# Retention and a squared-ReLU FFN in one kernel: fewer DMAs for q and for a tail's store, and retention clusters joined from the sixth group on

## The chip, the cores and the metric

The kernel runs on one core of a Trainium2 chip. The metric is the device time in microseconds (us) of one execution, as the median of several. The core has five engines that work side by side: TensorE (PE in the profile) for matrix products into PSUM, VectorE (DVE), ScalarE (ACT), GpSimd (POOL), and SyncE (SP), which here issues nearly all DMA transfers. Sixteen DMA engines move the data between device memory (DRAM) and on-chip memory (SBUF). "SPq" and "ACTq" in the profile are the DMA issues of SyncE and ScalarE.

## The reference

A causal retention (attention without softmax, with a decay per head) feeds a feed-forward network (FFN) whose nonlinearity is the square of ReLU.

```python
# q, k, v: (8 sequences, 8 heads, 576 positions, 64), float32
scores = scale * np.matmul(q, k.transpose(0, 1, 3, 2))
gamma = 1.0 - 2.0 ** (-5.0 - np.arange(H))
Dmat = np.where(rel >= 0, gamma[:, None, None] ** rel[None, :, :], 0.0)
attn_out = np.matmul(scores * Dmat[None], v)
# x: (4608, 512); w_in: (512, 2048); w_out: (2048, 512)
x = attn_out.transpose(0, 2, 1, 3).reshape(B * S, H * D)
h = x @ w_in
r = np.maximum(h, 0.0)
out = (r * r) @ w_out
```

## The kernel before

A sequence of 576 positions is four full chunks of 128 and a tail of 64. A *unit* is one full chunk of one sequence, or the tails of two sequences together, on the 128 partitions. There are 36 units, and a *group* is two of them; the 18 groups are numbered from 0. The last group (17) and group 8 consist of tails; all others of full chunks. Groups 0 to 3 are loaded and transposed in another way (`PAIRED = 8` units) and are not touched by the change.

The host-side scheduler takes tasks with an engine, a priority key, an assumed duration and dependencies, runs an event simulation, and writes the instructions in the order that comes out. The order on each engine is then fixed: what an assumed duration changes is only that order.

```python
for t in self.tasks: ...          # event simulation, then: for t in order: t["fn"]()

units = []                        # per pair of sequences: 8 full units; after every second pair: 2 tail units
sizes = [2] * 18                  # groups
JOIN = 7
sched = Schedule(dict(ff=8, prS=1, prO=1, g=3, ld=5, wst=4, kq=7, v16=7, rT=2, x=3, rl=3, o=4, ..., kqT=6))
```

Loading a unit, and its casts and transpose. The q of a full unit is laid out so that partition 32 x + r has four consecutive rows of heads x and x + 4; k and v have a row per partition.

```python
def add_load(u):
    for n, (name, src) in enumerate((("k", k), ("q", q), ("v", v))):
        def fn(name=name, src=src):
            x = ld.tile([P, H, D], FP32, ...)
            if kind == "full" and name == "q":
                for j in range(NP):                                   # NP = 4
                    nc.sync.dma_start(out=x[32 * j:32 * j + 32].rearrange("r (a t) d -> r a (t d)", a=2),
                                      in_=src[b, :, c * P:(c + 1) * P, :].rearrange("(a x) (r t) d -> x r a (t d)", a=2, t=4)[j])
            elif kind == "full":
                nc.sync.dma_start(out=x, in_=src[b, :, c * P:(c + 1) * P, :].rearrange("h p d -> p h d"))
            ...
        loaded[name, u] = dma_task(0, QL if name == "q" and kind == "full" else 1.2, fn, ...)   # QL = 0.8

ck = add("POOL", base, 0.65, fk, deps=[loaded["k", u]], acq=("kq",))      # casts to float16
cq = add("POOL", base + 1, 0.62, fq, deps=[loaded["q", u], ck])
cv = add("POOL", base + 2, 1.1, fv, deps=[loaded["v", u]] + tail, acq=("v16",))
def fx2():
    t = tile_of["kqT", u] = work.tile([P, 2 * NP, P], FP16, ..., bufs=6)
    nc.sync.dma_start_transpose(out=t, in_=tile_of["kq", u].rearrange("p x n -> p (x n)"))
T["kqT", u] = [add("SP", -1, 2.7, fx2, deps=[ck, cq], acq=("kqT",), after=3.0, lag=LAG_T)]
```

The retention of a group on PE, as quads of 64x64 matmuls. A group not joined has a cluster with its scores and its sums (the state that is carried on) and a later cluster with its outputs. From group `JOIN` on a cluster holds the first outputs of a group and the scores of the next, and another the sums of the next and the rest of the outputs.

```python
def joined(g):
    return JOIN <= g < last_g

if not joined(g - 1):
    def fa():
        emit_scores(g)
        emit_sums(g)
    t = add("PE", base + 3, ..., fa, deps=scores_deps(g) + sums_deps(g), acq=(...))
if joined(g):
    def f1():
        emit_out1(g)
        emit_scores(g + 1)
    def f2():
        first_waits.append(tile_of["masking", g + 1])
        emit_sums(g + 1)
        emit_out2(g)
    t1 = add("PE", base + 10, ..., f1, deps=out1_deps(g) + scores_deps(g + 1), acq=("prO", "prS", "ff", "ff", "ff", "ff"))
    t2 = add("PE", base + 30, ..., f2, deps=[t1] + T["masked", g] + T["masked", g + 1] + sums_deps(g + 1), ..., lag=PAUSE)
else:
    def fb():
        emit_out1(g)
        nc.tensor.drain()
        emit_out2(g)
    t = add("PE", base + 24, ..., fb, deps=T["masked", g] + out1_deps(g), acq=("prO", "ff", "ff"))
```

`JOIN` also sets the priority of a group's casts on GpSimd: `base_of(g) - L * (2 if g > JOIN else 1)`, an earlier key for the groups after it.

Group g needs, for its scores, the transposed k and q (`kqT`) of both its units. The FFN of a group is 64 matmuls of 128x256 for the first product and 56 for the second (seven block products per group, from group 1 on). Its output is stored so:

```python
def store(u, o, lo=0, hi=DM, eng=nc.sync):
    if kind == "full":
        eng.dma_start(out=out[r0:r0 + P, lo:hi], in_=o[:, lo:hi])
    else:
        for i in range(2):
            r0 = (b + i) * S + 512
            eng.dma_start(out=out[r0:r0 + 64, lo:hi], in_=o[i * 64:(i + 1) * 64, lo:hi])
```

In the last group each unit is stored in two halves of 256 columns as they are done, one half by ScalarE's queue and one by SyncE's; the two units give four such stores. In group 8 a unit is one store of all 512 columns, issued by SyncE.

Of the kernel before, what the change touches and what calls it, by code (L numbers as in the profile page):

```python
# [15 lines left out]
class Schedule:  # L16
# [7 lines left out]
    def add(self, eng, key, dur, fn, deps=(), acq=(), after=None, lag=0.0):  # L24
        t = dict(eng=eng, key=key, dur=dur, fn=fn, acq=acq, n=len(self.tasks), users=[], free=[], lag=lag,
                 left=len(deps), ready=0.0, lat=self.LAT[eng] if after is None else after)
        for d in deps:
            d["users"].append(t)
        self.tasks.append(t)
        return t  # L30
# [73 lines left out]
def kernel(  # L104
# [9 lines left out]
    nc = tc.nc  # L114
    B, H, S, D = q.shape
    DM, DFF = w_in.shape
    assert (B, H, S, D, DM, DFF) == (8, 8, 576, 64, 512, 2048)
    P = 128
    NP = H // 2
# [84 lines left out]
    for kind, pattern in (("tail", [[1, 64]]), ("full", [[1, 4], [4, 16]])):  # L204
        m = mask[kind] = const.tile([P, 64], FP16, name=f"mask_{kind}")
# [7 lines left out]
    for c in range(2):  # L213
        for e in range(2):
            m = mask2[c * 64:(c + 1) * 64, e]
# [17 lines left out]
    WT_KEY = 96  # L233
    URGENT = 40
    SQ_LATE = (1, 4, 6)
    JOIN = 7
    LAG = {"k4": 0.7, "q4": 0.5}
    LAG_T, LAG_O = 1.5, 5.0
    PAIRED = 8
# [3 lines left out]
    add = sched.add  # L243
# [34 lines left out]
    def dma_task(key, dur, fn, **kw):  # L278
        t = add("SP", key, dur, fn, deps=list(last_load), **kw)
        last_load[:] = [t]  # L280
        return t
# [8 lines left out]
    def add_load(u):  # L290
        kind, b, c = units[u]
        for n, (name, src) in enumerate((("k", k), ("q", q), ("v", v))):
            def fn(name=name, src=src):
                x = ld.tile([P, H, D], FP32, name=f"{name}32", tag=f"{name}32")
                tile_of[name + "32", u] = x
                if kind == "full" and name == "q":
                    for j in range(NP):
                        nc.sync.dma_start(out=x[32 * j:32 * j + 32].rearrange("r (a t) d -> r a (t d)", a=2),
                                          in_=src[b, :, c * P:(c + 1) * P, :].rearrange("(a x) (r t) d -> x r a (t d)", a=2, t=4)[j])
                elif kind == "full":  # L300
                    nc.sync.dma_start(out=x, in_=src[b, :, c * P:(c + 1) * P, :].rearrange("h p d -> p h d"))
                else:
                    for i in range(2):
                        nc.sync.dma_start(out=x[i * 64:(i + 1) * 64],
                                          in_=src[b + i, :, 512:576, :].rearrange("h p d -> p h d"))
            loaded[name, u] = dma_task(0, QL if name == "q" and kind == "full" else 1.2, fn, acq=("ld",) if n == 0 else ())
# [42 lines left out]
    T = {}  # L349
# [15 lines left out]
    def add_unit(u, base):  # L365

        kind, b, c = units[u]
        tail = [tail_dec] if kind == "tail" else []

        def sorted_cast(op, out_, in_):  # L370
            op(out=out_.rearrange("p (n b a d) -> p n b a d", n=2, b=2, a=2),  # L371
               in_=in_.rearrange("p (a n b) d -> p n b a d", n=2, a=2))

        def fk():
            t = tile_of["kq", u] = cast.tile([P, 2, H * D], FP16, name="kq16", tag="kq16")
            sorted_cast(nc.gpsimd.tensor_copy, t[:, 0], tile_of["k32", u])

        def fq():
            if kind == "tail":
                sorted_cast(nc.gpsimd.tensor_copy, tile_of["kq", u][:, 1], tile_of["q32", u])  # L380
            else:
                nc.gpsimd.tensor_copy(out=tile_of["kq", u][:, 1].rearrange("p (t a d) -> p a t d", t=4, a=2),  # L382
                                      in_=tile_of["q32", u].rearrange("p (a t) d -> p a t d", a=2))

        def fv():
            t = tile_of["v16", u] = cast.tile([P, H, D], FP16, name="v16", tag="v16")
            nc.gpsimd.tensor_tensor(  # L387
                out=t, in0=tile_of["v32", u],
                in1=vdec[kind].rearrange("p (h o) -> p h o", o=1).to_broadcast([P, H, D]), op=ALU.mult)
        ck = add("POOL", base, 0.65, fk, deps=[loaded["k", u]], acq=("kq",))  # L390
        cq = add("POOL", base + 1, 0.62, fq, deps=[loaded["q", u], ck])
        cv = add("POOL", base + 2, 1.1, fv, deps=[loaded["v", u]] + tail, acq=("v16",))
        for what, t in (("k", ck), ("v", cv)):
            for w in gate.get((what, u), []):
                sched.need(w, t)
        T["casts", u] = [ck, cq, cv]
        sched.free("ld", [ck, cq, cv])
        def fx2():
            t = tile_of["kqT", u] = work.tile([P, 2 * NP, P], FP16, name="kqT", tag="kqT", bufs=6)
            nc.sync.dma_start_transpose(out=t, in_=tile_of["kq", u].rearrange("p x n -> p (x n)"))  # L400
        T["kqT", u] = [add("SP", -1, 2.7, fx2, deps=[ck, cq], acq=("kqT",), after=3.0, lag=LAG_T)]

    def add_unit_pair(u, base):

# [180 lines left out]
    def units_of(g):  # L585
        return sorted(groups[g])
# [4 lines left out]
    def base_of(g):  # L591
        return (units_of(g)[0] - len(groups[g])) * L - EARLY
# [81 lines left out]
    def joined(g):  # L674

        return JOIN <= g < last_g

# [83 lines left out]
    def add_casts(g):  # L761
        for u in units_of(g):
            if u < PAIRED:
                if u % 2 == 0:
                    add_unit_pair(u, base_of(g) - 5)
                continue
            add_unit(u, base_of(g) - L * (2 if g > JOIN else 1) + 4 * (u - units_of(g)[0]))

# [72 lines left out]
    def store(u, o, lo=0, hi=DM, eng=nc.sync):  # L841
        kind, b, c = units[u]
        if kind == "full":
            r0 = b * S + c * P
            eng.dma_start(out=out[r0:r0 + P, lo:hi], in_=o[:, lo:hi])
        else:
            for i in range(2):
                r0 = (b + i) * S + 512
                eng.dma_start(out=out[r0:r0 + 64, lo:hi], in_=o[i * 64:(i + 1) * 64, lo:hi])


    T["ff2"] = []
# [4 lines left out]
    def add_ff(g):  # L857
# [49 lines left out]
        for s, u in enumerate(us):  # L907
            end = base2 + NF * (s + 1)
            f2 = []
            late = g == 0 and s == 1  # L910
            for fi in range(NF):
                def f(fi=fi, s=s, u=u):
                    if fi == 0:
                        tile_of["po", u] = ps_ff.tile([P, DM], FP32, name="po", tag="ff")
                    nc.tensor.matmul(tile_of["po", u], lhsT=tile_of["g", g][:, fi, s * P:(s + 1) * P],  # L915
                                     rhs=w_out16[:, fi, :], start=(fi == 0), stop=(fi == NF - 1))
                f2.append(add("PE", 95.9 + fi / 1000 if late else base2 + NF * s + fi, 0.216, f, deps=[sq[fi // nf]] + wcast[4 + fi // 4] + f2[-1:],
                              acq=("ff",) if fi == 0 else ()))

            def fo(u=u):  # L920
                tile_of["o", u] = o_pool.tile([P, DM], FP32, name="o", tag="o")
                nc.scalar.copy(out=tile_of["o", u], in_=tile_of["po", u])
            oc = add("ACT", end + 1, 0.59, fo, deps=[f2[-1]], acq=("o",))
            sched.free("ff", [oc])
            st = add("SP", -0.5, 0.7, lambda u=u: store(u, tile_of["o", u]), deps=[oc], after=2.5, lag=LAG_O)
            sched.free("o", [st])
            ends.append(f2[-1])
# [3 lines left out]
    def add_strassen(g, us, base, sq):  # L931
# [124 lines left out]
        for u, ds in ((uA, [d11, c12]), (uB, [d22, d21])):  # L1056
            if g < last_g:
                st = [add("SP", -0.5, 0.7, lambda u=u: store(u, o_tile(u)), deps=ds, after=2.5, lag=LAG_O if g < last_g - 1 else 0.0)]
            else:
                st = []  # L1060
                for d in ds:
                    lo = 0 if d in (d11, d21) else HM
                    eng = ("ACT", base + 25.1, 0.05) if d is d11 or d is d22 else ("SP", -0.5, 0.05)
                    st.append(add(*eng, lambda u=u, lo=lo, eng=eng: store(u, o_tile(u), lo, lo + HM,
                                                                          nc.scalar if eng[0] == "ACT" else nc.sync),
                                  deps=[d], after=2.5))
            sched.free("o", st)
# [44 lines left out]
```

## Time and profile before

| | |
|---|---|
| time, median of 3 | 291.18 us (290.39 to 291.36) |
| span of the profiled execution | 288.7 us |
| DMA from SP: `k`, 24 issues of 256 KB | 4.5 us to landing (median) |
| DMA from SP: `q`, 96 issues of 64 KB | 3.2 us |
| DMA from SP: `v`, 24 issues of 256 KB | 3.4 us |
| transposes `kqT`, 28 issues | 3.9 us |
| stores of full units, 32 issues of 256 KB | 2.8 us |
| stores of tails, 4 of 128 KB and 8 of 64 KB | 3.1 us and 2.0 to 2.1 us |
| read and written | 36.70 MB and 9.44 MB |

The page has the busy share of each engine, the span in 40 equal slices (each digit is a tenth of busy time; for DMA it is the mean over 16 engines), the chain of work that ended last, and groups of instructions by line. In a row of the order of time the columns are start, duration (both us), engine, line of the kernel, operation, `out<-in`, shape, and how many instructions were merged into the row. Matmuls are pipelined, so the duration of a row is longer than its share of the engine's time; the distance from one start to the next is what counts.

The loads of the units from 8 on begin at about 42 us and the last transpose is issued at 221.63 us; PE's last block of matmuls starts at 283.35 us.

### The profile page before, as it was taken

What the parts mean: (1) busy time and instruction counts of PE and PEld (TensorE: products, weight loads), DVE (VectorE), ACT (ScalarE), POOL (GpSimd) and SP (SyncE); (2) the same over time, 40 slices, a digit from 0 to 9 for tenths busy, and PEclk for the clock granted to TensorE, in tenths of its full rate; (3) what the DMA queues carried; (4) which work ended last, traced back from release to release, by engine and by line L of the source; (5) the groups of instructions that cost most, each with busy time, mean ns of one, the idle gap of its engine ahead of it and who ended that gap; (6) DMA issues with size and microseconds to landing.
All of it is one profiled execution on the core that took longest, in us unless ns stands there. A gap on an engine that the chain in (4) does not pass through costs nothing.

```text
span 288.7 us, 10134 instructions
## 1 busy us (share of the span) xinstructions
PE 281.2 (97%) x4346; PEld 236.3 (82%) x4346; DVE 175.6 (61%) x341; ACT 187.6 (65%) x363; POOL 86.2 (30%) x124
## 2 busy tenths in 40 slices
PE   7999999999999999999999999999999999999994
PEld 2568767888888888888888888888888888888883
DVE  3772389858564857647474665666557656265632
ACT  5559975767575767667676757584867585847830
POOL 5560045443505233433434135252515000000000
PEclk9999999999999999999999999999999999999999
DMA  7999999999998797999989798969979120102004
GB/s 200 275 208 206 248 290 270 175 235 161 224 210 220 164 215 174 218 207 209 191 203 214 173 180 221 218 157 254 195 181 191 57 75 2 73 2 75 0 9 138
DMA packets 122156, 49.94 MB, mean 173 GB/s; under 512 B 94720, under 2 KB 117760, under 8 KB 122112
## 3 DMA queue, kind: packets, MB, share of 16 engines
q1 hardware_dynamic: 117568, 44.84, 70.3%
q0 software_dynamic: 4224, 4.19, 8.8%
q8 instruction: 34, 0.56, 0.8%
q10 hardware_dynamic: 320, 0.26, 0.4%
q14 instruction: 10, 0.08, 0.1%
HBM read 36.70 MB, written 9.44 MB: 160 GB/s over the span
## 4 chain that ended last, share of the span: by engine, by line
PE 91%; DMA 3%; POOL 2%; issue 2%; DVE 0%; POOLq 0%; DVEq 0%
PE ph L875 44%; PE po L972 36%; PE psO L357 4%; DMA w_in<-in_moe_w_in_dram 3%; PE po L915 2%; PE psc L357 2%; PE psS L357 2%; PE psT L439 1%; POOL mask L216 0%; POOL vx L420 0%; POOL w_in L331 0%; DVE o L995 0%; POOL mask_full L208 0%; POOL mask_tail L208 0%; DVE p L1024 0%
## 5 line engine op out<-in xcount | busy, mean ns | idle before, releaser
L875 PE MATMUL ph<-xT,w_in 128*128 128x256 f16 x1152 | 138.4, 273 | 0.1
L875 PEld LDWEIGHTS <-w_in 128*128 128x128 f16 x1152 | 111.4, 98 | 14.5 <-DMA w_in<-in_moe_w_in_dram 0.4
L883 ACT ACTIVATE rl<-ph 128x512 f16<-128x512 f32 x144 | 84.4, 587 | 56.5 <-PE ph L875 54.0
L893 ACT ACTIVATE gT<-rl 128x512 f16<-128x512 f16 x118 | 74.4, 631 | 3.4
L972 PEld LDWEIGHTS <-gS 128*128 128x128 f16 x544 | 51.7, 98 | 6.5
L972 PE MATMUL po<-wT,gS 128*128 128x256 f16 x408 | 55.9, 273 | 0.0
L972 PEld LDWEIGHTS <-gT 128*128 128x128 f16 x408 | 39.7, 98 | 4.7
L945 DVE TENSOR_TENSOR gS<-gT,gS 128x512 f16<-128x512 f16 (+1 forms) x51 | 28.6, 561 | 19.1 <-ACT gT L893 18.5
L972 PE MATMUL po<-w_out,gT 128*128 128x256 f16 x272 | 36.7, 273 | 0.0
L387 POOL TENSOR_TENSOR v<-v,vdec_full 128x512 f16<-128x512 f32 x24 | 26.2, 1090 | 24.5 <-DMA v<-in_v_dram 22.8
L945 DVE TENSOR_TENSOR gS<-gT 128x1024 f16<-128x1024 f16 x34 | 26.1, 769 | 10.9 <-ACT gT L893 9.4
L371 POOL CAST kq<-k 128x512 f16<-128x512 f32 x28 | 18.5, 661 | 47.3 <-DMA k<-in_k_dram 43.2
L382 POOL CAST kq<-q 128x512 f16<-128x512 f32 x24 | 16.1, 670 | 31.7 <-DMA q<-in_q_dram 31.7
L895 DVE TENSOR_TENSOR gT<-rl 128x512 f16<-128x512 f16 x26 | 12.0, 462 | 22.0 <-ACT rl L883 22.0
L995 DVE TENSOR_TENSOR o<-po,u 128x256 f32<-128x256 f32 x33 | 13.9, 422 | 17.3 <-ACT u L985 8.6
L985 ACT COPY u<-po 128x256 f32<-128x256 f32 x34 | 12.5, 368 | 13.6 <-PE po L972 13.5
L751 DVE TENSOR_TENSOR xT<-psO,gam_full 128x512 f16<-128x512 f32 x28 | 18.0, 682 | 3.7 <-PE psO L357 3.6
L995 DVE TENSOR_TENSOR o<-po,p 128x256 f32<-128x256 f32 x18 | 7.6, 424 | 20.6 <-ACT u L985 11.5
L972 PE MATMUL po<-w_out,gS 128*128 128x256 f16 x136 | 17.8, 273 | 0.0
L972 PE MATMUL po<-wT,gT 128*128 128x256 f16 x136 | 17.6, 273 | 0.0
L692 DVE TENSOR_TENSOR rT<-psc,mask_full 128x512 f16<-128x512 f32 x24 | 15.8, 684 | 2.2 <-PE psc L357 2.1
L461 DVE TENSOR_TENSOR R<-stmp,dec 128x512 f16<-128x512 f32 (+1 forms) x18 | 12.1, 671 | 0.4
(82 smaller groups left out, 220.8 us busy)
## 6 DMA issues: line engine op xcount, KB each, us to landing
out_dram<-o SPq DMA_DIRECT2D x32, 256.0 KB, 2.8
k<-in_k_dram SPq DMA_DIRECT2D x24, 256.0 KB, 4.5
q<-in_q_dram SPq DMA_DIRECT2D x96, 64.0 KB, 3.2
v<-in_v_dram SPq DMA_DIRECT2D x24, 256.0 KB, 3.4
pair<-in_k_dram SPq DMA_DIRECT2D x4, 512.0 KB, 5.7
pair<-in_q_dram SPq DMA_DIRECT2D x4, 512.0 KB, 7.3
pair<-in_v_dram SPq DMA_DIRECT2D x4, 512.0 KB, 6.8
w_in<-in_moe_w_in_dram POOLq DMA_DIRECT2D x4, 512.0 KB, 8.9
```

The source lines that it names most:

```text
L357: t = nc.tensor.matmul(out_, lhsT=lhsT, rhs=rhs, start=start, stop=True, skip_group_check=True, tile_position=(64 * row, 64 * col))
L371: op(out=out_.rearrange("p (n b a d) -> p n b a d", n=2, b=2, a=2), in_=in_.rearrange("p (a n b) d -> p n b a d", n=2, a=2))
L382: nc.gpsimd.tensor_copy(out=tile_of["kq", u][:, 1].rearrange("p (t a d) -> p a t d", t=4, a=2), in_=tile_of["q32", u].rearrange("p (a t) d ...
L387: nc.gpsimd.tensor_tensor(out=t, in0=tile_of["v32", u], in1=vdec[kind].rearrange("p (h o) -> p h o", o=1).to_broadcast([P, H, D]), op=ALU. ...
L692: tile_of["masking", g] = nc.vector.tensor_tensor(out=tile_of["rT", g][:, :, a], in0=tile_of["psc", g][a].rearrange("p (s n i) -> p s n i" ...
L751: nc.vector.tensor_tensor(out=tile_of["x", g].rearrange("p n (s e i) -> p e (n s) i", s=n, e=2)[:, c], in0=y.rearrange("p (o t r) -> p o r ...
L875: nc.tensor.matmul(tile_of["ph", g, fb][:, j, :], lhsT=w_in16[:, m, fi * P:(fi + 1) * P], rhs=tile_of["x", g][:, m, :], start=(m == 0), st ...
L883: nc.scalar.activation(out=t, in_=tile_of["ph", g, fb], func=ACTF.Relu)
L893: nc.scalar.activation(out=t, in_=rl, func=ACTF.Square)
L945: nc.vector.tensor_tensor(out=tile_of["S", g][:, k, sl], in0=in0(sl), in1=in1(sl), op=op)
L972: nc.tensor.matmul(tile_of["pb", g, bank], lhsT=left(i), rhs=right[:, i, :], start=(start and i == 0), stop=(i == HF - 1), skip_group_chec ...
L995: nc.vector.tensor_tensor(out=o_tile(u)[:, half * HM:(half + 1) * HM], in0=bank(x), in1=tile_of[name, g], op=ALU.add)
```

## The change

It has four parts. A tail's store becomes one DMA over both sequences and all 128 partitions, where it was one for each sequence. The q of a full unit becomes two DMAs, one for each half of the heads and over all partitions, where it was four of 32 partitions and all heads; the layout in SBUF is the same. The joined clusters begin with group 5, the sixth, in place of group 7. And the scheduler counts 2.4 us in place of 2.7 for a transpose. It is meant to spare issues on the DMA queues, and to spare the dearer separate clusters on PE.

```diff
-    JOIN = 7
+    JOIN = 5
@@ add_load
                 if kind == "full" and name == "q":
-                    for j in range(NP):
-                        nc.sync.dma_start(out=x[32 * j:32 * j + 32].rearrange("r (a t) d -> r a (t d)", a=2),
-                                          in_=src[b, :, c * P:(c + 1) * P, :].rearrange("(a x) (r t) d -> x r a (t d)", a=2, t=4)[j])
+                    for a in range(2):
+                        nc.sync.dma_start(out=x[:, NP * a:NP * a + NP].rearrange("p t d -> p (t d)"),
+                                          in_=src[b, NP * a:NP * a + NP, c * P:(c + 1) * P, :].rearrange("x (r t) d -> x r (t d)", t=4))
@@ add_unit
-        T["kqT", u] = [add("SP", -1, 2.7, fx2, deps=[ck, cq], acq=("kqT",), after=3.0, lag=LAG_T)]
+        T["kqT", u] = [add("SP", -1, 2.4, fx2, deps=[ck, cq], acq=("kqT",), after=3.0, lag=LAG_T)]
@@ store
-            for i in range(2):
-                r0 = (b + i) * S + 512
-                eng.dma_start(out=out[r0:r0 + 64, lo:hi], in_=o[i * 64:(i + 1) * 64, lo:hi])
+            eng.dma_start(out=out.rearrange("(b s) m -> b s m", s=S)[b:b + 2, 512:576, lo:hi], in_=o[:, lo:hi])
```

## The prediction, made before the result was known

> **What bounds the kernel now.** I read the page first: the share of each engine and the 40 slices.
>
> ```profile
> PE 281.2 (97%) x4346; PEld 236.3 (82%) x4346; DVE 175.6 (61%) x341; ACT 187.6 (65%) x363; POOL 86.2 (30%) x124
> ...
> PE   7999999999999999999999999999999999999994
> ...
> DMA  7999999999998797999989798969979120102004
> ...
> PE 91%; DMA 3%; POOL 2%; issue 2%; DVE 0%; POOLq 0%; DVEq 0%
> ```
>
> TensorE is full from the second slice to the last, and the chain of waits is 91% TensorE. A busy PE need not be at its peak, so I checked the order of time on PE. In the FFN blocks 20 matmuls of 128x256 start 2.18 us before the next block does, 109 ns each, and nearly every block follows the last one at that pace, from 17.7 us to 284.2 us. So only three things can move the end: what PE has to do, a wait put into its stream, and what comes after its last matmul. The DMA row is the second thing to see: about 9 tenths up to slice 31, nearly nothing after it. Loads run ahead of PE, but not at leisure.
>
> Second, the retention clusters on PE, in the order of time. Here a cluster of scores and sums that stands by itself (two L357 lines), then the FFN blocks on both sides of the same group's output cluster (its many short lines are left out):
>
> ```profile
> 90.73 1.04 PE L972 MATMUL po<-wT,gS 128*128 128x256 f16 x8
> 91.70 0.44 PE L357 MATMUL psc<-kqT 64*64 64x64 f16 x32
> 91.97 0.46 PE L357 MATMUL psS<-v,kq 64*64 64x64 f16 x32
> 92.37 0.61 PE L972 MATMUL po<-wT,gS 128*128 128x256 f16 x4
> ...
> 95.00 2.35 PE L875 MATMUL ph<-xT,w_in 128*128 128x256 f16 x20
> ...
> 98.20 1.05 PE L972 MATMUL po<-wT,gS 128*128 128x256 f16 x8
> ```
>
> 90.73 plus 8 x 0.109 is 91.60, and the next FFN block starts at 92.37: the scores and sums cost 0.77 us. 95.00 plus 20 x 0.109 is 97.18, next block 98.20: the outputs cost 1.02 us. A joined group, by the same sum, costs 0.60 (cluster at 154.35) plus 0.87 (at 158.46).
>
> Third, the end, and the stores of the last group, from the DMA view of 283 to 288 us and the order of time after 284 us:
>
> ```profile
> DMA  0005960049889301794006954989849620000000
> ...
> q10 hardware_dynamic: 320, 0.26, 21.5%
> ...
> out_dram<-o ACTq DMA_DIRECT2D x4, 64.0 KB, 2.1
> ```
>
> ```profile
> 284.46 0.42 DVE L995 TENSOR_TENSOR o<-po,p 128x256 f32<-128x256 f32 x1
> 284.92 1.10 SPq L849 DMA_DIRECT2D out_dram<-o  x2
> ```
>
> The last add ends at 284.88, two stores are issued in 1.10 us, the last packet is written by about 287.1 (33 slices of 0.125 us), and the span ends at 288.7. The row q10 is the tail stores issued by ACT: 256 packets of 1 KB and 64 tiny ones in 21.5% of 16 engines x 5 us = 17.2 us, so about 67 ns of one DMA engine for each KB. A full store's 2 KB packets take 87 ns by the same sum over 281 to 283 us (69.5% of 32 us by 256).
>
> [...] about 0.1 us lies between a full-array block and the 64x64 quads (91.60 to 91.70).
>
> **The change, part by part.**
>
> JOIN from 7 to 5 turns the outputs of groups 5 and 6 and the scores of groups 6 and 7 from separate clusters into joined ones. Removed: 2 x (0.77 + 1.02) = 3.58 us. Added: 2 x (0.60 + 0.87) = 2.94 us. PE saves 0.6 us. All on the path, since PE is full.
>
> The transposes' shorter count (2.7 to 2.4) changes no instruction, only the order that the host-side scheduler writes. In the joined part the score clusters already stand where their keys want them or earlier, so I expect little from it: 0, with a risk that PE is sent to a transpose a little sooner.
>
> The tail store: by intention it saves one issue at the end, 0.5 us. But its DRAM side is now (2 sequences, 64 rows, 256 columns): the slowest size is 2, against 128 partitions in SBUF. [...] The last group has four such stores (two halves of two units) of 128 packets of 1 KB each, so each of two engines gets 256 packets where each of 16 had 32. At 67 ns that is 17.2 us; at the rate of the 2 KB packets (43 ns a KB) 11.1 us; I take 14. The first of these stores puts out its data at 283.3 (the first busy slice), 0.6 us earlier after the change: 282.7 + 14 = 296.7 in place of 287.1. That is +9.6 us (6.7 to 12.8), with PE's saving in it. DMA is on the path there; nothing hides it.
>
> The tail stores of group 8 (about 160 us) carry rows of 2 KB, 64 packets for each of two engines per unit: 2 x 64 x 87 ns = 11.1 us, in place of 1.4. What stands behind them in those two rings waits up to 9.7 us.
>
> The q loads: the DRAM side is now (4 heads, 32 row groups, 1 KB), slowest size 4, so k is 4. A unit's 256 packets go to four engines, 64 each, where it was 16 each. SP gains: four issues took 2.0 to 2.4 us of some 6 us of SP's time per unit, two would take about 1.0 (an estimate, from the 0.43 to 0.58 us of a k or v issue). The four engines lose. From 102.77 to 115.16 us, one period of loads, the SP queue's packets took 86.8% of 16 engines, 10.8 us per engine for two units. q is 32 packets of that at about 57 ns (54.1% of 16 us by 183 packets, 36 of them tiny, from 59.5 to 60.5 us): 1.8 us. So [...] 9.0 + 128 x 0.057 = 16.3 us of packets per group, all others 9.0. These times overlap (the share reaches 1.13 over 22 to 58 us), which makes about 14.4. PE takes 13.9 us for a group (score clusters from 113.48 to 238.40 us, nine groups). So four DMA engines become about as full as PE. Slack before PE waits is 6 us at group 10 (last transpose issued 131.16, landing 3.9 later, scores at 141.10) and 12.8 at the last group. With the 9.7 us of group 8's stores in two of these rings I expect stalls of about 4 us, between 0 and 12, first near 166 to 180 us.
>
> Sum: 291.2 + 9.6 + 4 = 304.8 if k falls [...] (I give that nearly 9 in 10); 290.0 if it does not (291.2 - 0.6 - 0.5). I lean to the lower part of the first[...]: 302.
>
> **The rivals.** *The change does what it means to*: all DMAs still use 16 engines, SP issues less, PE saves 0.6 and the end 0.5: 290.0. For it: the four-way q and two-way stores look like plain overhead in the SP rows. Against it: the slowest sizes of 4 and 2, and that the old form puts 32 and 64 outermost on both sides. *Only the end gets longer*: the loads run far enough ahead that four fuller engines never stop PE: 298 to 301. For it: 6 to 12.8 us of slack, and SP's relief. [...] at 16.3 us per group against 13.9 over a dozen groups, less the slack, PE would stand still for some 15 to 20 us: 315 to 320. Against it: the overlap in those busy times. *The earlier joined cluster of group 5 waits*: the transpose that it needs was issued at 78.33, landing 82.3, and its key puts it near 83.7; a stall of 0 to 3 us there.
>
> **Range and chances.** The low end, 294, [...] for packets quicker than any seen here; the high end, 311, is the 67-ns end (304) with 7 us of stalls. Slower by 2% means over 297.0: nearly every case with k of 2 at the end, 0.81. Within 2%: [...] packets quicker than any seen here, 0.17. Faster by 2% would need 5.8 us, and the parts meant to save have 1.1: 0.02.
>
> **What would show it.** In the changed profile: the tail's stores take many us from issue to landing where they had 2.1, and the row of DMA at the end is 1 to 2 tenths for 10 us or more (two of 16 engines), after PE's last matmul. q's landing grows from 3.2 us[...]. PE has the two separate pairs of clusters near 82 to 107 us replaced, 0.6 us less in sum. Stalls would be gaps on PE ahead of score clusters, with the transposes of that group landing just before. The prediction is wrong if the stores land in some 2 us (then 290), or if PE shows gaps in every group from about 85 us on (then over 311).

## The result and the profile after

The changed kernel takes 322.8 us (median of 4, 321.41 to 323.47) against 291.1 us for the kernel before in the same runs: a ratio of 1.1087, 95% interval 1.1041 to 1.1133. It is slower, by about the means that the prediction names, and by three times as much: +31.7 us where +11 was predicted, and outside the range of 294 to 311.

The page of the changed kernel, the lines that answer to those of before, with the clock, the row of ACT's tail stores and the chain by lines added:

```profile
PE 287.6 (90%) x4346; PEld 239.6 (75%) x4346; DVE 175.8 (55%) x341; ACT 187.5 (59%) x363; POOL 88.0 (28%) x124
...
PE   8999999999779999697999992988999999999940
...
PEclk9999999999979999899999996899999999999995
DMA  7999998999979899799989688496959960110021
...
q1 hardware_dynamic: 116104, 44.84, 68.8%
...
q10 hardware_dynamic: 260, 0.26, 0.2%
...
PE 37%; SPq 24%; DMA 20%; POOL 6%; issue 3%; DVE 3%; ACT 2%; POOLq 0%; DVEq 0%
PE ph L873 16%; PE po L970 13%; DMA q<-in_q_dram 13%; SPq L298 12%; SPq L301 7%; DMA kqT<-kq 4%; SPq L400 3%; DMA v<-in_v_dram 3%; PE po L913 2%; POOL kq L382 2%; POOL v L387 2%; PE psO L357 2%; SPq L845 1%; PE psc L357 1%; ACT rl L881 1%
```

Three things are to be seen. The PE row has holes (7, 6, 2) from slice 10 on, and an end of two slices (4, 0) without matmuls. The chain that ended last is 37% PE where it was 91%: now it runs through the loading of q (`DMA q` 13%) and SP's issuing of q, k and v (`L298`, `L301`). And the packet counts tell of the DMA engines. ACT's tail stores (row q10) were 256 packets of data and 64 tiny ones, 16 for each of four DMAs; now they are 256 and 4, two for each of two DMAs. From 308 to 316 us, where only tail stores run, the DMA share is 0.13, two of 16 engines. So I read one tiny packet for each engine that a DMA uses. In row q1 the kernel before has 117568 packets and this one 1464 fewer. With q on 4 engines that should be 96 x 16 - 48 x 4 = 1344, and with SP's eight tail stores of before on 16 engines made four on 2, 8 x 16 - 4 x 2 = 120; together 1464, to the packet. So by this reading the number of engines that share a transfer, the prediction's k, is 4 for q and 2 for a tail's store, as their slowest sizes are, where it was 16 with sizes of 32 and 64; which ones of the 16 they are, the counts do not tell.

Waits of the changed kernel (engine, line, what it waited for: us in total, times, the longest):

```profile
POOL kq L382 <- DMA q<-in_q_dram: 88.9, 24, 9.4
...
PEld L357 <- DMA kqT<-kq: 18.0, 9, 5.8
PE psc L357 <- DMA kqT<-kq: 17.0, 9, 5.7
```

GpSimd's cast of q waits 88.9 us for q's load (31.7 before), the transposes come as late as that, and PE's score clusters wait 17.0 us for transposed keys and queries; the kernel before has no such row. The order of time on PE, at the first stall and at the longest:

```profile
87.04 0.32 PE L357 MATMUL psc<-kqT 64*64 64x64 f16 x16 [1.11 <-DMA kqT<-kq]
89.62 0.43 PE L357 MATMUL psc<-kqT 64*64 64x64 f16 x16 [2.26 <-DMA kqT<-kq]
89.98 1.04 PE L970 MATMUL po<-w_out,gS 128*128 128x256 f16 x4
90.81 1.84 PE L970 MATMUL po<-wT,gT 128*128 128x256 f16 x8
92.49 2.35 PE L873 MATMUL ph<-xT,w_in 128*128 128x256 f16 x20
...
198.29 0.43 PE L357 MATMUL psc<-kqT 64*64 64x64 f16 x16 [5.69 <-DMA kqT<-kq]
```

The first stall is in group 5's joined cluster at 85.6 us, not at 166 to 180. In all, ten score clusters from there to 231 us (a cluster is timed from its first 64x64 matmul to the next FFN matmul) take 24.2 us in place of 10 x 0.51 = 5.1: 19.1 us of stalls, in eight of the ten. After a long gap comes a second loss: eight matmuls from 90.81 to 92.49 take 0.21 us each in place of 0.109. More on that below.

SP's order of time where the long stall begins:

```profile
188.02 0.61 SPq L847 DMA_DIRECT2D out_dram<-o  x1
188.69 0.46 SPq L301 DMA_DIRECT2D k<-in_k_dram  x1
189.27 6.83 SPq L400 DMA_TRANSPOSE kqT<-kq  x1
196.19 0.60 SPq L847 DMA_DIRECT2D out_dram<-o  x1
```

These `L847` are group 8's tail stores, now on two engines. SP is held for 6.83 us in the issue of the transpose behind one of them, and PE waits 5.69 us for just this transpose. Last, the end, in the DMA view of 300 to 320 us:

```profile
DMA  0000010076940111011111111111111111110000
...
q10 hardware_dynamic: 260, 0.26, 3.7%
```

From the 16th of 40 slices to the 36th, each of 0.5 us, about a tenth of 16 engines is busy, as two engines would be. 3.7% of 16 x 20 us is 11.8 us of engine time for the 256 packets of 1 KB that ACT issued: 46 ns each. SP issued as many, so each of the two engines has 256 of them. PE's last block starts at 306.18 us, 22.8 later than before (283.35), and the rest of the span after that block's start grew from 5.3 to 13.5 us, by 8.2.

### The profile page after: what moved, and what is told of

It reads as the page before. It is cut to its first block, busy times and chain, and to the rows that moved or that the text cites. A ratio compares the mean times of both kernels' runs of the same rounds, so it can differ in the third digit from the quotient of the medians.

```text
span 319.7 us, 10052 instructions
## 1 busy us (share of the span) xinstructions
PE 287.6 (90%) x4346; PEld 239.6 (75%) x4346; DVE 175.8 (55%) x341; ACT 187.5 (59%) x363; POOL 88.0 (28%) x124
## 4 chain that ended last, share of the span: by engine, by line
PE 37%; SPq 24%; DMA 20%; POOL 6%; issue 3%; DVE 3%; ACT 2%; POOLq 0%; DVEq 0%
PE ph L873 16%; PE po L970 13%; DMA q<-in_q_dram 13%; SPq L298 12%; SPq L301 7%; DMA kqT<-kq 4%; SPq L400 3%; DMA v<-in_v_dram 3%; PE po L913 2%; POOL kq L382 2%; POOL v L387 2%; PE psO L357 2%; SPq L845 1%; PE psc L357 1%; ACT rl L881 1%
## 5 line engine op out<-in xcount | busy, mean ns | idle before, releaser
L970 PE MATMUL po<-wT,gS 128*128 128x256 f16 x408 | 57.1, 277 | 0.0
L943 DVE TENSOR_TENSOR gS<-gT,gS 128x512 f16<-128x512 f16 (+1 forms) x51 | 29.9, 587 | 23.8 <-ACT gT L891 23.2
L382 POOL CAST kq<-q 128x512 f16<-128x512 f32 x24 | 17.1, 714 | 88.9 <-DMA q<-in_q_dram 88.9
L387 POOL TENSOR_TENSOR v<-v,vdec_full 128x512 f16<-128x512 f32 x24 | 27.6, 1150 | 9.0 <-DMA v<-in_v_dram 8.0
L692 DVE TENSOR_TENSOR rT<-psc,mask_full 128x512 f16<-128x512 f32 x24 | 15.6, 684 | 22.1 <-PE psc L357 22.1
L357 PE MATMUL psc<-kqT 64*64 64x64 f16 (+1 forms) x576 | 11.5, 205 | 17.1 <-DMA kqT<-kq 17.0
L993 DVE TENSOR_TENSOR o<-po,u 128x256 f32<-128x256 f32 x33 | 13.9, 422 | 17.2 <-PE po L970 10.1
L357 PEld LDWEIGHTS <-kqT 64*64 64x64 f16 x576 | 8.3, 111 | 20.0 <-DMA kqT<-kq 18.0
L893 DVE TENSOR_TENSOR gT<-rl 128x512 f16<-128x512 f16 x26 | 11.0, 423 | 21.7 <-ACT rl L881 21.7
L970 PE MATMUL po<-wT,gT 128*128 128x256 f16 x136 | 18.4, 281 | 0.3 <-DVE o L993 0.3
```

The lines of the kernel that those rows point to most:

```text
L357: t = nc.tensor.matmul(out_, lhsT=lhsT, rhs=rhs, start=start, stop=True, skip_group_check=True, tile_position=(64 * row, 64 * col))
L387: nc.gpsimd.tensor_tensor(out=t, in0=tile_of["v32", u], in1=vdec[kind].rearrange("p (h o) -> p h o", o=1).to_broadcast([P, H, D]), op=ALU. ...
L943: nc.vector.tensor_tensor(out=tile_of["S", g][:, k, sl], in0=in0(sl), in1=in1(sl), op=op)
L970: nc.tensor.matmul(tile_of["pb", g, bank], lhsT=left(i), rhs=right[:, i, :], start=(start and i == 0), stop=(i == HF - 1), skip_group_chec ...
L993: nc.vector.tensor_tensor(out=o_tile(u)[:, half * HM:(half + 1) * HM], in0=bank(x), in1=tile_of[name, g], op=ALU.add)
```

## The experiments

The theory after the result: q's loads on four engines make the chain load, cast, transpose slower than PE needs it, for most of the kernel, and tail stores on two engines add the end and one hold in the middle. Rivals: the order of instructions (the joined clusters, or the short count of an SP task) is to blame rather than the rate of the four engines; a fixed latency of q rather than a rate; one of the stores alone makes the long stall. The kernel before took 290.4 to 290.6 us beside these runs.

**q as before, the rest of the change kept** (`e1_q_four`):

```diff
-                    for a in range(2):
-                        nc.sync.dma_start(out=x[:, NP * a:NP * a + NP]..., in_=src[b, NP * a:NP * a + NP, ...]...)
+                    for j in range(NP):
+                        nc.sync.dma_start(out=x[32 * j:32 * j + 32]..., in_=src[...]...[j])
```

> The changed kernel with q again in four DMAs over 16 engines; the one-piece tail stores, JOIN 5 and the shorter transpose count stay. Engines theory (the narrow DMAs cost the time, each by itself): 291.1 - 0.6 for the joined clusters + 8.2 at the end + the part of the stall at 192 to 217 us that group 8's stores make (up to 8 us, perhaps 5) = 304, range 299 to 307; no stall of PE before 160 us. Order theory (the scheduler now puts score clusters ahead of their transposes, whatever the DMAs): stalls at 85, 130 and 146 us stay, 310 or more.

Measured: 300.2 us, ratio 1.0334 (1.0291 to 1.0376). Nearly all stalls are gone:

```profile
PEld L357 <- DMA kqT<-kq: 0.6, 2, 0.3
PE psc L357 <- DMA kqT<-kq: 0.3, 2, 0.2
```

So the two kinds of tail stores with the joined clusters are worth +9.6 us, and q the other 22.6.

**The tail stores as before, q on four engines kept** (`e2_store_two`): the store's line of the change put back to two DMAs of 64 partitions.

> The changed kernel with the tails' stores again in two DMAs each; q stays in two DMAs on four engines. Engines theory: the end is short again (4.5 us from PE's last matmul to the end of the span, not 12.6), the stall near 192 us shrinks to the 2 to 4 us of its neighbours, the stalls at 85, 130 and 146 us stay: 322.8 - 8.2 - 5 = 309 (305 to 314). If q's four engines cost little and the stores nearly all: 296 or less.

Measured: 310.8 us, 1.0667 (1.0611 to 1.0722). q costs +20.2 us by itself, here with the joined clusters; PE again stalls from 85.4 us on. +20.2 and +9.6 make 29.8 of the 31.7: the parts nearly add up, and some 2 us come of their meeting.

**Both put back: only the joined clusters and the shorter count remain** (`e3_both_back`).

> The kernel before with only JOIN 5 and the transpose count of 2.4: all DMAs over 16 engines. Engines theory: 290.5 (291.1 - 0.6), no stalls. Order theory: slower than before by most of the 31.7 us; anything over 295 means that the order alone does harm.

Measured: 290.4 us, 1.0004 (0.9989 to 1.0018). On PE the four clusters of groups 5 and 6 take 2.58 us (0.50, 0.78, 0.51, 0.79) where those of before took 3.19, the 0.6 us of the prediction, but PE is 0.4 us late by group 5's scores (77.14 us against 76.74), and the whole shows no difference. There is no stall: joined clusters from group 5 on harm nothing while the loads are on 16 engines. They do ask for the transposes earlier: by a landing 3.9 us after the issue, groups 6 to 11 have 1.8 to 2.6 us of slack here, where they had 4.7 to 11.8 in the kernel before.

**q in two DMAs, but on 16 engines** (`e4_q_two_wide`): the version above with the row groups outermost in q's load, so that the slowest size is 32 and not 4; PE then reads the transposed q with a step of 4 elements.

```diff
-    ... in_=src[b, NP * a:NP * a + NP, ...].rearrange("x (r t) d -> x r (t d)", t=4)
+    ... in_=src[b, NP * a:NP * a + NP, ...].rearrange("x (r t) d -> r x (t d)", t=4)
-    ... else t[:, :, 32 * x + 16 * c:32 * x + 16 * c + 16]
+    ... else t.rearrange("p t (r x) -> p x t r", x=NP)[:, x, :, 16 * c:16 * c + 16]
```

> As the one with both DMA parts undone, but q in two DMAs whose slowest size is 32 row groups (partition 4 r + x in place of 32 x + r, and PE reads the transposed q with a step of 4), so 16 engines each: same number of issues as the changed kernel. Engines theory: as e3_both_back within 0.5 us, about 290.5, q's issue time on SP down by about half. If two large DMAs, not few engines, did the harm: stalls at 85 to 150 us come back, 305 or more. If the step of 4 slows PE's reading: up to 1 us slower with longer score clusters.

Measured: 294.7 us, 1.0139 (1.0120 to 1.0158). Its row q1 has 116800 packets, 768 fewer than before: 96 x 16 - 48 x 16, so 16 engines for each DMA. PE never waits for a transpose. Two DMAs for q are thus not what stalls PE; two DMAs on four engines each are. The 4.3 us that it lost all the same were not expected, and they are in the clusters. PE's groups of one shape, in the kernel with both put back and then in this one (busy time, mean ns of one):

```profile
L357 PE MATMUL psO<-kqT,Rm 64*64 64x64 f16 x192 | 9.1, 195 | 0.0
...
L357 PE MATMUL psc<-kqT 64*64 64x64 f16 x448 | 6.2, 194 | 0.0
```

```profile
L357 PE MATMUL psO<-kqT,Rm 64*64 64x64 f16 x192 | 11.2, 228 | 0.0
...
L357 PE MATMUL psc<-kqT 64*64 64x64 f16 x448 | 9.1, 228 | 0.0
```

Clusters with scores take 0.82 us in place of 0.51 and those with the rest of the outputs 0.87 in place of 0.78: 0.4 us by 11 joined groups is 4.4 us. (There are twelve; the q of tails is read without the step.)

**Only q on four engines, all else as before** (`e5_q_narrow_only`): clusters joined from group 7, the count 2.7.

> The kernel before with only q in two DMAs of slowest size 4 (JOIN 7, transposes counted 2.7, tail stores in two). Rate theory [...]: the later, separate clusters only add a few us of slack, 305 to 309, gaps before score clusters as in the run with the stores undone (310.8). Order theory (JOIN 5 and the count of 2.4 turned a small delay into stalls): 299 or less.

Measured: 303.8 us, 1.0419 (1.0357 to 1.0480), between the two theories. The order counts for something: without the earlier joined clusters q costs 13 us in place of 20, and PE's first stall is at 113 us. But most of the loss is there without them.

**The scheduler told that q's issue is long** (`e6_q_counted_3us`): `e2_store_two` with `QL`, the assumed time of q's load on SP, 3.0 in place of 0.8.

> The run with the stores undone (310.8: q on four engines, JOIN 5, count 2.4), but the scheduler counts 3.0 us for a unit's q in place of 0.8, so that it writes score clusters later in PE's order and FFN work before them. Rate theory: the time hardly moves, 305 to 312, since work for PE runs out behind the loads. Order theory: PE finds FFN work in the gaps, 296 or less.

Measured: 306.9 us, 1.0568 (1.0548 to 1.0588). A better informed order wins back 4 of 20 us. In its profile PE no longer waits for a transpose at all, and still has 19.1 us without work (304.2 - 285.1), where the kernel before has 7.5 (288.7 - 281.2). The waits, none over 1.5 us, are now for other steps of the same groups:

```profile
PE po L972 <- DVE gS L945: 3.3, 6, 1.0
PE ph L875 <- DVE xT L751: 3.2, 5, 1.5
```

The transposes still come 15.5 us apart (241.27 less 55.59, by 12). Thus the new order moves the clusters to where their data is, but does not bring the data sooner. Whether the loads or the order itself hold this version to its pace was not separated: its chain that ended last is 78% PE.

**q on two engines** (`e7_q_two_engines`): `e2_store_two` with each of q's two DMAs cut into two, of two heads each, so that the slowest size is 2. It issues four DMAs per unit, as the kernel before does.

```diff
                     for a in range(2):
+                        for j in range(2):
-    ... x[:, NP * a:NP * a + NP] ... src[b, NP * a:NP * a + NP, ...]
+    ... x[64 * j:64 * j + 64, NP * a:NP * a + NP] ... src[b, NP * a + 2 * j:NP * a + 2 * j + 2, ...]
```

> The run with the stores undone (310.8), but q in four DMAs of slowest size 2, so that all of a unit's q runs on two engines: 128 packets of 1 KB on each, 5.9 us at 46 ns where it was 2.9. Rate theory: the loads of a group take 15 + 5.9 = 20.9 us and the whole about 365 us (345 to 380). If only the number of engines in a DMA and not their load mattered (a fixed latency per DMA): 311 to 320.

Measured: 359.5 us, 1.2373 (1.2329 to 1.2417). The rate theory said 365, a fixed latency at most 320. That these DMAs are on two engines is read from the tail's stores of the same slowest size (two tiny packets each), not from their own packets. The waits:

```profile
POOL kq L383 <- DMA q<-in_q_dram: 141.4, 24, 8.0
PEld L358 <- DMA kqT<-kq: 48.3, 22, 6.9
PE psc L358 <- DMA kqT<-kq: 45.4, 21, 6.8
```

PE now waits in nearly every group. The cost is a rate of the few engines: four issues a unit on two engines (359.5 us) cost far more than two issues on four (310.8), and two on 16 (294.7, `e4_q_two_wide`) stall nothing.

**q issued by GpSimd** (`e8_q_from_gpsimd`): `e2_store_two` with q's two DMAs issued from GpSimd. It was to tell whether the cost comes of SP's DMAs falling on the same four engines each time.

> The run with the stores undone (310.8), with the same two q DMAs issued by GpSimd. [...] Theory of the same four engines: [...] no or small gaps, 291 to 296 (GpSimd spends about 0.9 us on an issue, it is 30% busy). If a narrow DMA is slow as such: 305 or more.

Measured: 335.6 and 338.3 us, a ratio of 1.1598 (1.1541 to 1.1656); two further executions took 342.3 and 344.3 us, and the profile is of the first of these. This is a miss, and settles nothing about which engines are used: GpSimd issues q in the order of its own instructions, among casts that wait 110.9 us for q, and the issues themselves cost it 32.8 us. Its packets do not show a group of four either (6912 more on GpSimd's queue: 48 x 128 of data and 48 x 16 tiny ones). Whether it matters that the same engines get every q stays open.

```profile
L298 POOL DMA_DIRECT2D q<-in_q_dram x48 | 32.8, 686 | 0.4 <-issue 0.3
...
q<-in_q_dram POOLq DMA_DIRECT2D x48, 128.0 KB, 5.7
```

**Only the last group's half stores in one DMA** (`e9_end_store_one`): everything else as before.

```diff
+            if hi - lo < DM:
+                eng.dma_start(out=out.rearrange("(b s) m -> b s m", s=S)[b:b + 2, 512:576, lo:hi], in_=o[:, lo:hi])
+            else:
                 for i in range(2): ...    # as before
```

> The kernel before, with only the last group's half stores (256 of 512 columns) made one DMA instead of two; q, the clusters and group 8's tail stores stay as they were. If the end term of the prediction is right in kind, nothing moves before the last FFN blocks, and the end takes 256 packets of 1 KB on each of two engines: by the changed kernel's 46 ns a packet 11.8 us, so PE's last matmul to the end of the span grows from 4.5 to about 12.6 us: 299 us (297 to 301). A rival that puts the longer end on the loads still in flight from q would leave it below 294.

Measured: 298.6 us, 1.0278 (1.0251 to 1.0306): +8.2 us. Its DMA view of 282 to 298 us (slices of 0.4 us):

```profile
DMA  8800111111111111101111111111111110000000
...
q10 hardware_dynamic: 260, 0.26, 4.6%
```

Again 11.8 us (4.6% of 16 x 16 us) for 256 packets. PE's last block starts at 283.18 us, as in the kernel before. The end term stands alone, and does not need q.

**Only group 8's tail stores in one DMA** (`e10_group8_store_one`): the same edit with the condition `hi - lo == DM`.

> The kernel before, with only group 8's tail stores (all 512 columns) made one DMA instead of two. By the first theory (the store holds two rings for 6 to 10 us, and only a chain of loads without slack passes that on) the transpose behind it comes later, one load period is some 20 us long, and PE, whose loads run ahead here, waits 0 to 2 us: 291 to 293 us. By the rival (the store alone makes the stall of 5.7 us that the changed kernel shows at 192 us) it is 296 to 298.

Measured: 292.4 us, 1.0064 (1.0039 to 1.0089): some 1.9 us by this ratio, and PE's last block starts 1.8 us later (285.18 us), in place of the 5 to 6 that the rival had. The load period with these stores is 22.4 us long, much as in the changed kernel (23.9), but PE has one wait for a transpose, of 1.4 us. +8.2 and +1.8 about make up the +9.6 of the first experiment.

**A version for use** (`e11_stores_on_both_queues`): the kernel before with the joined clusters and the shorter count, and the last group's half stores still two DMAs on all 16 engines, one issued by SP and one by ACT.

```diff
-                eng.dma_start(out=out[r0:r0 + 64, lo:hi], in_=o[i * 64:(i + 1) * 64, lo:hi])
+                (nc.scalar if hi - lo < DM and i else nc.sync).dma_start(out=out[r0:r0 + 64, lo:hi], in_=o[...])
```

> The kernel before with the two intended gains that the runs left standing or possible: joined clusters from group 5 on (0.6 us less on PE) and the transposes' shorter count, and the last group's half stores still two DMAs over all 16 engines, but one issued by SP and one by ACT instead of both by the same queue, so that the second issue (0.5 us) does not lie behind the first at the end. Expected: PE's last matmul to the end of the span some 0.45 us shorter than the 4.5 of the kernel before; 289.5 to 290.3 us against 290.6. If ACT's own work or DMA packets set the end instead, no difference to the version with both parts undone (290.4).

Measured: 289.9 us against 290.4 us over 22 executions: 0.9980 (0.9971 to 0.9990). It is half a microsecond better than the kernel before. From the start of PE's last block to the end of the span it takes 5.2 us (283.05 to 288.2) where the version with both parts put back takes 5.3 (283.31 to 288.6), less of a saving than expected; how the rest of the half microsecond divides between the end and the clusters was not separated.

## Why the prediction was wrong, step by step

**The number of engines: right.** Four for q and two for a tail's store, by the packet counts.

**Joined clusters: right in size** (0.6 us on PE), too small to be seen in the whole. The shorter count was not tried alone.

**The end: right in kind, somewhat too long.** I took 14 us for 256 packets on each of two engines; it is 11.8 (46 ns a packet, not 54), and +8.2 us where the sum had 10.2 (its +9.6 has 0.6 saved by PE in it).

**Group 8's stores: right that they hold what is issued behind them, undecided in what it costs.** In an otherwise unchanged kernel a transpose behind them comes 7.4 us later (9.7 at most by the prediction) and the whole takes 1.8 us more; in the changed one, with no slack left, they make its longest stall, and cost 3.8 us (322.8 less the 310.8 without either store, less 8.2 for the end).

**q: this is the step that failed.** The prediction put it so: "Slack before PE waits is 6 us at group 10 (...) and 12.8 at the last group. With the 9.7 us of group 8's stores in two of these rings I expect stalls of about 4 us". The rate of loads was well worked out: about 14.4 us per group. With only q changed, the second transposes of groups are issued 14.5 us apart on average over twelve periods (229.1 less 55.5, by 12). What was wrong is what this was compared with. I held 14.4 against PE's 13.9 and had half a microsecond per group to pay, out of a slack read from the kernel before as if it were a stock. But that slack is made on the way: in the kernel before loads take 12.8 us per group and PE 13.9, and so the slack grows by about 1 us per group on average, from 6.0 to 12.8 over the last seven, though not evenly (5.6 at group 13, behind group 8's stores). Slower loads do not use up this reserve; they never build it. The loss per group is 14.4 less 12.8.

The sum that fits takes the delay of the loads at one late point, subtracts the slack that the kernel before has there, and has PE's delay. The point is the last transpose of the last group but one of those loaded. In the kernel before, and in the changed one, SP's rows there read:

```profile
207.02 2.31 SPq L400 DMA_TRANSPOSE kqT<-kq  x1
```

```profile
243.00 1.24 SPq L400 DMA_TRANSPOSE kqT<-kq  x1
```

In the kernel before this lands 3.9 us later, at 210.9, and the score cluster begins at 223.80: 12.9 us of slack. The same for the other kernels (us):

| kernel | load period, mean of 12 | issued later than before | less the slack of 12.9 | PE's last block, measured later |
|---|---|---|---|---|
| only q on four engines (`e5`) | 14.5 | 22.1 | 9.2 | 10.1 |
| with joined clusters and count (`e2`) | 15.3 | 33.2 | 20.3 | 20.4 |
| the change | 15.6 | 36.0 | 23.1 | 22.8 |
| q on two engines (`e7`) | 18.9 | 80.3 | 67.4 | 68.1 |

The periods and PE's delay are those of the profiled executions. The fourth column agrees with the last within 1 us, over a range of 60 us. This is an account made after the runs: the loads' delay is itself measured, and PE's stalls may be in it. It shows that PE's delay is the loads' delay less the slack, not why the loads are late; for that stand `e1_q_four`, `e4_q_two_wide`, `e5_q_narrow_only` and `e7_q_two_engines`. The same sum explains group 8's stores alone: the transpose comes 7.4 us later than before (178.0 against 170.6), the slack there is 180.05 - 174.5 = 5.6, which leaves 1.8 us; measured 1.8. With the prediction's own figures it would have been 12 x (14.4 - 12.8) = 19.2, and 9.7 of group 8, less 12.9: stalls of 16 us in place of 4, and 317 us.

The rest of the miss is in the period. It is 15.3 and not 14.5 us once the clusters are joined from group 5 and the count is shorter. 0.3 us of this is there without a stall (13.1 in `e3` against 12.8 before). That PE's stalls hold buffers which the next loads need would explain the rest, but that was not tried, and which of the two edits does it stays open. A KB packet's place in the period can be read from three kernels that differ in q's DMAs alone (four of 16 engines for a unit, two of four, four of two): 13.1 us with 32 packets of q per engine and group (`e3`), 15.3 with 128 (`e2`), 18.9 with 256 (`e7`), if q falls on the same engines each time, which was not shown. That is an estimated 23 and 28 ns a packet, about half of the 57 ns of busy time per packet in the prediction, which fits the overlap that it allowed for.

**The rivals.** The third, with PE standing still for "some 15 to 20 us: 315 to 320", came nearest, and was set aside for the overlap, which speaks for a lower rate but not for the slack. "Only the end gets longer" is what `e9_end_store_one` shows by itself. The earlier joined cluster of group 5, put at 0 to 3 us, does wait, 3.9 us, but only when q is slow (`e3_both_back` has no wait there, though only 2.6 us of slack). The leaning towards the lower part was right for the packets of the end (46 ns against 67) and had no bearing on q.

**What would show it** was well chosen: "gaps on PE ahead of score clusters, with the transposes of that group landing just before" is just what the order of time has, from 85 us on, nearly as the case "over 311" said (eight groups of ten, not every one).

## What to carry to other kernels

Before merging DMAs, write down the slowest dimension of both sides: here sizes of 4 and 2 put these DMAs on 4 and 2 engines by their packet counts, one saved issue of 0.5 us at the end cost 8.2 us, and two saved issues per unit cost 13 to 20. Slack behind a producer that runs ahead is made on the way at the difference of two rates, so compare the new rate of the producer with its own old rate, carry the delay to a late point, and only then subtract the slack found there. Where the slack is nearly gone, expect a second change to cost more than it would alone: here the earlier use of the transposes cost nothing by itself and 7 us with the slow q (310.8 against 303.8), and the hold by group 8's stores 1.8 by itself and 3.8 with it.

## What the runs showed of the hardware that was not expected

**TensorE at half clock after a long gap.** Windows of the changed kernel after the longest stall (window, its us, busy us and instructions of PE, PEld, DVE, ACT, POOL, then the granted clock, the DMA share and GB/s):

```profile
199.00:200.00 1.00, 1.00 (x7) 0.70 (x5) 1.00 (x3) 0.00 (x0) 0.00 (x0) 0.50 0.25 78
200.00:201.00 1.00, 1.00 (x7) 0.69 (x6) 0.97 (x4) 0.42 (x1) 0.00 (x0) 0.50 0.25 83
201.00:202.00 1.00, 1.00 (x8) 0.78 (x7) 1.00 (x2) 0.81 (x2) 0.00 (x0) 0.66 0.25 86
202.00:203.00 1.00, 1.00 (x12) 0.90 (x10) 0.04 (x1) 0.49 (x1) 0.00 (x0) 1.00 0.97 242
```

PE is at work again from 198.29 us, and the clock is 0.50 for three more us; a mean of 0.66 from 201 to 202 means that it came back at about 201.7. That is 3.4 us at half speed, an estimated 1.7 us lost on top of the gap. By the same reading the stalls at 86 and 131 us cost 1.4 and 1.5 us more, while the one at 214 us, of 2.4 us, left the clock at 1.00. PE's delay of 22.8 us, with the 0.6 saved, less 19.1 of stalls leaves 4.3 us; the three recoveries sum to 4.6.

In slices of 0.2 us the clock falls or rises at 89.03, 92.44, 133.41, 136.82, 194.84 and 201.67 us, and the distances are 1, 12, 1, 17 and 2 times 3.41 us. In the 3.41 us before the three falls PE was busy for 0.6, 1.1 and 1.2 us, so in this run gaps well below 3.4 us were enough (2.6 us at 131). The one at 214 us, after which the clock stayed at 1.00, falls into two stretches of the same 3.41 us grid, each with PE busy for over half of it (2.7 and 1.8 us). That fits a gap's place on the grid counting as well as its length, but this was not tried.

**A step of four elements on PE's operand is not free.** 228 ns in place of 194 for a 64x64 fp16 matmul that reads q with a step of 8 bytes (`e4_q_two_wide`). Matmuls of the same shape that do not read q stayed at 195 ns in this run (`psO<-rT,v`, `psS<-v,kq`).

**Fewer engines, shorter packets.** A 1 KB packet of a tail store took 67 ns of its engine with 16 engines at work and 46 with two. What makes the packets shorter was not tried.
